# A prefetch hint for the branch that skips the fallback path of a gated-recurrence and feed-forward kernel

## The chip, the core and the metric

The kernel runs on one core of one Trainium2 chip. The metric is the device time of one execution in microseconds. A comparison of two kernels uses the median of several executions of each. The profiled execution is one more execution, recorded instruction by instruction, and has a time of its own.

## What is computed

The reference has two parts. The first is a gated linear recurrence over 768 steps for 4 batches of 8 heads with 48 channels, with a complex gate per step and channel. The second is a feed-forward block on the 3072 rows that result.

```python
def _attn_ref(q, k, v, a_re, a_im):
    mag = np.sqrt(a_re * a_re + a_im * a_im)
    scale = np.minimum(mag, 0.999) / (mag + 1e-06)
    a_re_n, a_im_n = (a_re * scale, a_im * scale)
    for t in range(S):
        ar, ai = (a_re_n[:, :, t, :, None], a_im_n[:, :, t, :, None])
        new_re = ar * S_re - ai * S_im
        new_im = ar * S_im + ai * S_re
        kv = np.einsum('bhd,bhe->bhde', k[:, :, t], v[:, :, t])
        S_re, S_im = (new_re + kv, new_im)
        y[:, :, t] = np.einsum('bhd,bhde->bhe', q[:, :, t], S_re)

def _moe_ref(x, w_in, w_out):          # x: 3072 x 384, w_in: 384 x 2048, w_out: 2048 x 384
    h = x @ w_in
    g = h * (1.0 / (1.0 + np.exp(-h)))
    return (g @ w_out).astype(np.float32)
```

## The kernel before, in words

**Tiling.** The sequence is cut into 24 chunks of 128 steps (6 for each of the 4 batches), and these are handled in 12 pairs. Inside a chunk the recurrence is turned into matrix products: the gates are brought into logarithm and angle, summed along the chunk, and applied to q and k. Then come the products of q and k (L501), the state carried to the next chunk (L574), and the output of the chunk (L525, L528). Each pair gives 256 rows for the feed-forward block. `hidden` (L591) computes the hidden layer in eight groups. `result_of_halves` (L677) multiplies it by the second weight, in a form with seven products of half size for each pair of blocks. VectorE forms sums of the hidden layer for that (L620).

**Order.** The first pairs are written out by hand. The later ones run through `step`, which follows a string of letters, inside a region in which every engine issues its instructions in the order written (`tc.manual_schedule`, L943 and the lines after). Where the instructions written outside that region fall among those inside it is left to the scheduler. The last step, p = 12, has no further chunk to prepare. It computes only the last pair's hidden layer and result, and between these it loads the small parts of the weights that `look` inspects (`small`, L240, and `looked_at`, L247).

**The very end of the arithmetic.** `result_of_halves` ends with one copy on ScalarE (L685), seven adds on VectorE (L689) and three stores to the output: one from SP's queue, one from ScalarE's queue, and a second from SP's queue (all L648).

**The fallback and its branch.** The fast form works only if the decays and the weights are not too small. Behind the region of ordered steps the kernel reduces both to a flag. `low` (L952, L954) is taken from the decays, `fit` (L956, L957) from the weights. Two small DMAs put both in one row (L959, L960), a third reduction gives `weak` (L962), and all five engines load the flag into a register (L964). `tc.If` at L965 runs `step_by_step`, a slow exact path, if the flag is zero. With the inputs of the reference it is not zero, and every engine branches over that code to the end of the program. The skipped code has loops and transfers on SP, VectorE, ScalarE and TensorE, and little on GpSimd. Behind it are only the closing semaphore operations and barriers, which the profile gives the lines L965 and L1119.

```python
    weak = consts.tile([1, 1], I32)
    nc.vector.tensor_reduce(out=weak, in_=all_, op=ALU.min, axis=mybir.AxisListType.X)
    fast.close()
    ok = nc.values_load(weak[0:1, 0:1], min_val=0, max_val=1)
    with tc.If(ok < 1):
        step_by_step(ctx, tc, q, k, v, a_re, a_im, w_in, w_out, w1, w2, out)
```

Of the kernel before, what the change touches and what calls it, by code (L numbers as in the profile page):

```python
# [60 lines left out]
def kernel(  # L61
# [886 lines left out]
            step(p, parts(hidden, p - 1), parts(result, p - 1), order)  # L948


    low = consts.tile([D2, 1], F32)
    nc.vector.tensor_reduce(out=low, in_=decs.rearrange("p n h -> p (n h)"), op=ALU.min,  # L952
                            axis=mybir.AxisListType.X)
# [7 lines left out]
    weak = consts.tile([1, 1], I32)  # L961
    nc.vector.tensor_reduce(out=weak, in_=all_, op=ALU.min, axis=mybir.AxisListType.X)  # L962
    fast.close()
    ok = nc.values_load(weak[0:1, 0:1], min_val=0, max_val=1)  # L964
    with tc.If(ok < 1):  # L965
        step_by_step(ctx, tc, q, k, v, a_re, a_im, w_in, w_out, w1, w2, out)


# [155 lines left out]
```

## Time and profile before

| what | us |
|---|---|
| median of 5 executions | 674.1 |
| lowest and highest of the 5 | 673.02 and 676.2 |
| the profiled execution's own time | 671.09 |
| its span, first to last instruction | 669.3 |
| TensorE busy (matmul) | 638.8 |
| VectorE, ScalarE, GpSimd busy | 454.7, 345.5, 166.8 |
| mean granted TensorE clock | 0.989 of full speed |

In the profile PE is the matmul side of TensorE, PEld its weight loads, DVE is VectorE, ACT ScalarE, POOL GpSimd and SP SyncE. A name with a q behind it (SPq, PEldq) is that engine's sequencer, which handles register, branch, semaphore and DMA-issuing instructions; these are not counted as busy time. The span leaves out what lies before the first and after the last recorded instruction; for this execution that is 1.8 us. Times of single instructions count from the start of the span.

### The profile page before, as it was taken

To read this page: it belongs to the slowest core of one execution; us is meant where nothing else is said; L and a number is where in the kernel's file an instruction comes from. 1 tells how busy PE (TensorE), PEld (TensorE's weight loads), DVE (VectorE), ACT (ScalarE), POOL (GpSimd) and SP (SyncE) were. 2 spreads that over 40 slices of the span, in tenths; PEclk is the share of its full clock that TensorE was granted. 3 is DMA by queue.
4 is the path that set the end of the run, shared out by engine and by line. 5 is a ranking of instruction groups with operands and counts; after the bars stand their busy time and mean duration, and the time that the engine had idled before them with its cause. 6 is when DMAs were issued, how large, how long until landed. Compare 5 with 4: busy or idle time off the path is not lost.

```text
span 669.3 us, 11275 instructions
## 1 busy us (share of the span) xinstructions
PE 638.8 (95%) x4066; PEld 569.9 (85%) x4066; DVE 454.7 (68%) x979; ACT 345.5 (52%) x526; POOL 166.8 (25%) x256
## 2 busy tenths in 40 slices
PE   5688999999999999999999999999999999998995
PEld 3476877577899999999999999999999999997995
DVE  3786736849785784784784784785785785864532
ACT  7779634655862672671681681780780681510110
POOL 7474201250320330230240240240240240230000
PEclk8899999999999999999999999999999999999998
DMA  9968658181294184194185185176176174577730
GB/s 170 226 141 183 147 151 187 39 132 28 42 136 67 36 131 77 35 133 75 30 131 82 33 121 93 31 113 101 30 104 111 32 96 71 195 159 221 232 105 29
DMA packets 171632, 71.20 MB, mean 106 GB/s; under 512 B 155920, under 2 KB 160144, under 8 KB 171568
## 3 DMA queue, kind: packets, MB, share of 16 engines
q1 hardware_dynamic: 158448, 49.76, 37.3%
q0 software_dynamic: 8768, 15.92, 15.7%
q10 hardware_dynamic: 4352, 4.72, 2.1%
q8 instruction: 34, 0.56, 0.3%
q14 instruction: 30, 0.25, 0.1%
HBM read 48.86 MB, written 4.79 MB: 80 GB/s over the span
## 4 chain that ended last, share of the span: by engine, by line
PE 83%; DVE 4%; ACT 4%; DMA 4%; SPq 2%; issue 1%; POOL 0%; DVEq 0%; ACTq 0%
PE h L591 34%; PE o L677 27%; PE a L501 5%; PE o L633 4%; PE s L574 4%; PE y L525 3%; PE y L528 3%; DMA raw<-in_moe_w_in_dram 2%; DMA T<-sq 1%; SPq L492 1%; PE phase L390 1%; ACT s L295 1%; ACT T L483 1%; PE L L390 1%; ACT cs L295 1%
## 5 line engine op out<-in xcount | busy, mean ns | idle before, releaser
L591 PE MATMUL h<-xT,w 128*128 128x256 f32 x1152 | 260.1, 380 | 1.1 <-ACT xT L565 1.1
L591 PEld LDWEIGHTS h<-xT,w 128*128 128x128 f32 x1152 | 216.4, 190 | 29.6 <-ACT xT L565 1.7
L295 ACT ACTIVATE g<-h 128x512 f32<-128x512 f32 x96 | 55.5, 596 | 167.4 <-PE h L591 161.3
L492 POOL DMA_DIRECT2D T<-sq x120 | 77.1, 650 | 65.7 <-issue 56.2
L290 ACT ACT_TABLE_LOAD x64 | 82.1, 1283 | 2.5 <-PEq L1108 1.3
L677 PE MATMUL o<-w,gs 128*128 128x192 f32 x320 | 77.8, 326 | 0.0
L506 DVE TENSOR_TENSOR w<-a,upto_r 128x512 f32<-128x512 f32 x48 | 32.7, 687 | 60.2 <-PE a L501 60.2
L542 POOL DMA_DIRECT2D xT<-y x30 | 15.9, 535 | 213.2 <-ACT y L538 194.2
L677 PE MATMUL o<-w,g 128*128 128x192 f32 x320 | 66.6, 331 | 0.0
L677 PE MATMUL o<-wc,gs 128*128 128x192 f32 x320 | 64.9, 326 | 0.0
L534 ACT COPY xT<-y 128x384 f32<-128x384 f32 x20 | 9.6, 479 | 101.9 <-PE y L528 101.9
L677 PEld LDWEIGHTS o<-w,g 128*128 128x128 f32 x320 | 53.8, 190 | 3.5 <-issue 1.9
L677 PEld LDWEIGHTS o<-w,gs 128*128 128x128 f32 x320 | 56.3, 190 | 0.0
L501 PEld LDWEIGHTS a<-T 96*128 96x128 f32 x384 | 49.1, 192 | 7.4 <-issue 3.2
L677 PEld LDWEIGHTS o<-wc,gs 128*128 128x128 f32 x320 | 54.2, 190 | 0.0
L501 PE MATMUL a<-T 96*128 96x128 f32 x384 | 50.2, 276 | 4.0 <-DMA T<-sq 2.6
L440 POOL DMA_DIRECT2D decs<-ends x48 | 30.5, 641 | 90.8 <-DMA ends<-eq 89.9
L620 DVE TENSOR_TENSOR gs<-g 128x128 f32<-128x128 f32 x160 | 38.6, 282 | 20.9 <-PE o L677 12.8
L633 PE MATMUL o<-w,g 128*128 128x384 f32 x128 | 42.6, 488 | 0.0
L677 PE MATMUL o<-wc,g 128*128 128x192 f32 x160 | 38.9, 326 | 0.0
L633 PEld LDWEIGHTS o<-w,g 128*128 128x128 f32 x128 | 24.2, 190 | 16.1 <-issue 0.2
L525 PE MATMUL y<-w,v 128*64 128x128 f32 x320 | 35.2, 282 | 0.0
(106 smaller groups left out, 947.2 us busy)
## 6 DMA issues: line engine op xcount, KB each, us to landing
T<-sq SPq DMA_DIRECT2D x120, 64.0 KB
T<-sq POOLq DMA_DIRECT2D x120, 64.0 KB, 4.1
raw<-in_moe_w_out_dram SPq DMA_DIRECT2D x16, 384.0 KB
small<-in_moe_w_in_dram SPq DMA_DIRECT2D x16, 384.0 KB
small<-in_moe_w_out_dram SPq DMA_DIRECT2D x16, 384.0 KB
raw<-in_moe_w_in_dram SPq DMA_DIRECT2D x24, 192.0 KB
out_dram<-ot ACTq DMA_DIRECT2D x23, 192.0 KB
q<-in_q_dram SPq DMA_DIRECT2D x18, 192.0 KB
```

What stands on the lines that cost most here:

```text
L290: chain(nc.scalar.preload_act_table_set({"exp": "natural_log_exp_and_others", "trig": "trig_and_small", "silu": "silu_and_others"}[of]))
L295: chain(nc.scalar.activation(out=out, in_=in_, func=func, **kw))
L440: nc.gpsimd.dma_start(out=decs[a * D:(a + 1) * D, n], in_=ends[n].rearrange("(h d) -> d h", d=D))
L492: (nc.gpsimd if a % 2 else nc.sync).dma_start(out=to[ts(b, Q), :, a], in_=sq[ts(a, Q), b])
L501: nc.tensor.matmul(ps[:, h], lhsT=x["kT"][:, hh * HH + h], rhs=x["qT"][:, hh * HH + h], start=True, stop=True)
L506: nc.vector.tensor_tensor(out=x["w", hh], in0=ps, in1=upto.unsqueeze(1).to_broadcast([C, HH, C]), op=ALU.mult)
L525: nc.tensor.matmul(to, lhsT=v_[:, cols], rhs=x["w", h // HH][:, h % HH], start=True, stop=not carried)
L574: nc.tensor.matmul(ps[:, h], lhsT=x["kr"][:, h].rearrange("p c d -> p (c d)"), rhs=x["v"][:, h], start=True, stop=True)
L591: nc.tensor.matmul(ps[:, ji], lhsT=w1[:, dc, ts(jp * 2 + ji, C)], rhs=A[p]["xT"][:, dc], start=(dc == 0), stop=(dc == ND - 1))
L620: nc.vector.tensor_tensor(out=t[:, i], in0=a, in1=b, op=op)
L633: nc.tensor.matmul(A[p]["o"][m].rearrange("p n c -> p (n c)"), lhsT=A[p]["g", jp][:, ji, ts(m, C)], rhs=w2[:, j], start=(j == 0), stop=(j ...
L677: nc.tensor.matmul(o[i], lhsT=a, rhs=b, start=(jp == 0 and i < 4), stop=(final and j == jp and i in ((5, 3, 6, 2) if p == NP - 1 else (4, ...
```

## The change

A call ahead of the reductions marks a place for a branch hint under the name "weak", of the kind "LikelyTaken", on four engines: SP, VectorE, ScalarE and TensorE. The branch of the `If` gets the same name as its label, which ties the two together: at the marked place each of the four engines gets an instruction that names its branch at L965 as one that will probably be taken. GpSimd gets none. Nothing else differs.

```diff
+    tc.mark_branch_hint_location("weak", "LikelyTaken", (
+        mybir.EngineType.SP, mybir.EngineType.DVE, mybir.EngineType.Activation,
+        mybir.EngineType.PE))
     low = consts.tile([D2, 1], F32)
     nc.vector.tensor_reduce(out=low, in_=decs.rearrange("p n h -> p (n h)"), op=ALU.min,
                             axis=mybir.AxisListType.X)
...
     ok = nc.values_load(weak[0:1, 0:1], min_val=0, max_val=1)
-    with tc.If(ok < 1):
+    with tc.If(ok < 1, label="weak"):
         step_by_step(ctx, tc, q, k, v, a_re, a_im, w_in, w_out, w1, w2, out)
```

## The prediction

> **What bounds the kernel now.** I read the page first, then the chain of waits, then the instructions of the two lines at the branch (L964 reads the flag, L965 jumps), then the DMA queues in short stretches around them. From the page:
>
> ```profile
> span 669.3 us, 11275 instructions
> ...
> PE 638.8 (95%) x4066; PEld 569.9 (85%) x4066; DVE 454.7 (68%) x979; ACT 345.5 (52%) x526; POOL 166.8 (25%) x256
> ...
> PE 83%; DVE 4%; ACT 4%; DMA 4%; SPq 2%; issue 1%; POOL 0%; DVEq 0%; ACTq 0%
> ```
>
> TensorE bounds the body, and the change removes no matmul. But its last matmul ends at about 662.4 us and the last VectorE add (L689) at 662.8, while the span ends at 669.3. So 6.5 us lie behind the arithmetic, and the change can act only there. The answer for L965 shows what fills them (columns: engine and operation, count, min/median/max ns, first and last start):
>
> ```profile
> L965 SPq EVENT_SEMAPHORE  x8: 17/17/17, 667.0 to 667.6; - x8
> L965 POOLq COMPARE_BRANCH  x1: 62/62/62, 649.8 to 649.8; - x1
> L965 POOLq EVENT_SEMAPHORE  x1: 17/17/17, 650.3 to 650.3; - x1
> L965 PEldq COMPARE_BRANCH  x1: 3622/3622/3622, 659.9 to 659.9; - x1
> L965 DVEq COMPARE_BRANCH  x1: 72/72/72, 663.1 to 663.1; - x1
> L965 SPq COMPARE_BRANCH  x1: 45/45/45, 663.2 to 663.2; - x1
> L965 ACTq COMPARE_BRANCH  x1: 54/54/54, 663.4 to 663.4; - x1
> ...
> L965 DVEq EVENT_SEMAPHORE  x1: 21/21/21, 666.9 to 666.9; - x1
> L965 ACTq EVENT_SEMAPHORE  x1: 17/17/17, 667.0 to 667.0; - x1
> ```
>
> DVE, SP and ACT branch at 663.1, 663.2 and 663.4, and none issues its next instruction before 666.9 to 667.0: 3.5 to 3.8 us of nothing. TensorE shows the same length inside its branch (3622 ns), but 3.5 us earlier, beside its own queued matmuls. POOL, whose part of the skipped code is small, goes on after 0.5 us. The waits of SP's queue name the same gap, and the DMA answer for 664 to 665 us shows what happens in it:
>
> ```profile
> SPq L965 <- SPq L965: 3.8, 1, 3.8
> ```
>
> ```profile
> DMA  8996864310000700900007000000000000000000
> ...
> q1 hardware_dynamic: 80, 0.05, 16.0%
> q14 instruction: 3, 0.02, 7.3%
> q8 instruction: 1, 0.02, 6.3%
> ```
>
> Each digit of the DMA line is 25 ns. The stores' last data are gone by 664.23; at 664.33 to 664.53 three packets of the instruction queue follow, one for each of the three waiting engines. I read the gap as each engine fetching the code at the branch's target. TensorE's single packet (queue q8) at 661.2 fits too: 1.3 us after its branch, and 2.3 us before it goes on at 663.5.
>
> [...] the branches here took 45 to 72 ns, and I use those. [...] the 0.5 KB transfer of `fit` ended its issue at 647.36, moved data until 648.2, and its reader `weak` started at 648.80. [...]
>
> **The change, part by part.** Nothing is removed or moved in the arithmetic, no wait is added, no DMA is issued by the kernel. Two edits:
>
> 1. The label on the `If`: no instruction, cost nothing.
>
> 2. Four hint instructions, one each on SP, DVE, ACT and PE. No row of before shows one. The nearest rows are single sequencer instructions: a MOVE takes 29 to 42 ns (L1108), L964's register operation 196 ns and its load of the flag 474 to 572 ns. So one hint costs between 0.03 and 0.6 us of its own sequencer; I take 0.1. On PE the sequencer runs ahead of the array (its flag load is at 659.3, the last matmul begins at 662.1), and SP, DVE and ACT idle between their instructions for microseconds at a time. With that cover gone, on DVE behind the last add, it would be 0.1, at most 0.6.
>
> What the hint can take away is the 3.5 to 3.8 us on three engines. All three must lose it, as they resume together. The branch then costs what POOL's costs, 0.5 us from its start to the next instruction: ACT, the latest, is through at 663.4 + 0.5 = 663.9 instead of 667.0, so 3.1 us are the ceiling.
>
> What is late next: the output stores. SP issues the last one at 662.82 for 0.35 us, its data end at 664.23, and SP must see it landed before the kernel may end. The receipt is not visible, because SP arrives too late to wait for it. Two estimates: data end plus the 0.6 us seen for `fit` gives 664.8[...]. I take 665.0. Behind it stand SP's eight semaphore instructions of L965 (667.0 to 667.6) and the closing barrier of L1119 (667.7 to 669.3, 1.6 to 1.7 us). If the wait for the store is the first of the eight, the remaining 2.3 us follow it: end 667.3, gain 2.0. If it is the last, 1.7 us follow: end 666.7, gain 2.6. If it stands later, in the closing barrier, the gain nears 3.1. I take **2.4 us**: span 666.9, and the profiled execution, 671.09 us with 1.8 us around its span, becomes 668.7. The median of the five runs stands 3.0 us above the profiled execution, at 674.1; the same 2.4 us off it gives **671.7 us**, 0.36% less. About 0.3%, or 2.0 us, is what a measurement of this kernel can tell from no change.
>
> The open term is whether the hint acts in time: it must be executed before its engine needs the block, some 3.6 us ahead. In the source it stands behind the ordered steps. It depends on no data, and the trace shows that such code is moved up: `low` (L952), written just behind it, ran at 586.4, between instructions of those steps, as soon as its data were there. Against it, the flag loads, ready at 649.2, sit at 662.4 on DVE and 662.8 on ACT, behind all other work.
>
> **The rivals.**
>
> *Too late or without effect: no change.* If DVE executes its hint just before its flag load at 662.4, the fetch starts there: 662.4 + 3.6 = 666.0 instead of 666.9, gain 0.8; ACT, at 662.8, gains 0.6 and, being the slower, sets it. If nothing is fetched the gain is 0. Median 673.5 to 674.1. For it: the late flag loads, and a gain that needs three engines at once. Against it: `low` moved up by 76 us.
>
> *The hint displaces the block needed next: slower.* If a hint executed early makes the engine fetch the far target at once in place of the code that follows, the engine misses its own next block, 3.6 us, and the target is gone again by the end. Place: VectorE or ScalarE in the start-up, where the chain passes through them; a miss on TensorE is partly covered by the 2.8 us its sequencer was ahead. One uncovered miss: 674.1 + 3.6 = 677.7. It decides from where under 1.6 us of it is hidden. [...] Against it: the code between hint and branch is straight, and a hint names a branch, so it has reason to act only near that.
>
> *The stores bind harder.* Receipts of 2.5 us behind the data would leave an end like today's: gain 0 to 1.5, inside the no-change case.
>
> **How the numbers follow.** In time and effective: 0.62, of which 0.07 ends at a gain under 2.0 us. Too late, without effect, or bound by the stores: 0.27. Displacing: 0.11. That gives faster by over 0.3% 0.55, within 0.3% 0.34, slower 0.11. The likeliest case's own range is a gain of 2.0 to 3.1, 671.0 to 672.1, and medians of five runs that reach from 673.0 to 676.2 may stand a microsecond off: 670.0 to 673.1. The 80% range adds the no-change case with the same spread above it and leaves out most of the slower one: 670.0 to 675.3.
>
> **What the profile after would show.** Right: four new sequencer instructions well before 655 us; PE's branch far under 3622 ns; DVE, SP and ACT with 0.5 us or less from branch to next instruction; SP's L965 group beginning near 663.7 and stretched by a wait for the store until about 665.0; the closing barrier as long as now; the three instruction packets before 663. Too late: hints at 662 and the gap merely shorter. Displaced: a new idle stretch of 3 to 4 us in an engine's sequencer near its hint, and the gap at L965 unchanged. The prediction is wrong if the gap goes and the span doesn't fall by 2 us, or if the span falls elsewhere than behind 662.8.

## The result and the profile after

The changed kernel takes 670.1 us (median of 23 executions), the kernel before 673.45 us (median of 44). The ratio is 0.9946, 95% interval 0.9932 to 0.9961, so 3.6 us are gone (2.6 to 4.6); the two medians themselves lie 3.3 us apart. The forecast was a gain of 2.4 us.

The line numbers of the end have moved by three: the flag loads are L967, the branch L968, the closing barrier L1122. The answer for L968 of the changed kernel (engine and operation, count, min/median/max ns, first and last start) stands against the one for L965 in the prediction:

```profile
L968 SPq EVENT_SEMAPHORE  x8: 17/17/17, 666.3 to 667.6; - x8
...
L968 PEldq COMPARE_BRANCH  x1: 393/393/393, 662.5 to 662.5; - x1
...
L968 DVEq COMPARE_BRANCH  x1: 84/84/84, 665.7 to 665.7; - x1
L968 SPq COMPARE_BRANCH  x1: 70/70/70, 665.8 to 665.8; - x1
L968 ACTq COMPARE_BRANCH  x1: 68/68/68, 665.9 to 665.9; - x1
L968 DVEq EVENT_SEMAPHORE  x1: 21/21/21, 666.3 to 666.3; - x1
L968 ACTq EVENT_SEMAPHORE  x1: 17/17/17, 666.4 to 666.4; - x1
```

TensorE's branch went from 3622 to 393 ns, and DVE, SP and ACT go on 0.5 to 0.6 us after the start of their branches instead of 3.7 to 3.8. SP's eight semaphore instructions now stretch over 1.2 us instead of 0.6. The waits of SP's queue say why (columns: total us, number of waits, the longest):

```profile
SPq L968 <- SPq L968: 1.4, 3, 0.6
```

The first of the three is the rest of the branch, 0.5 us. The other two stand ahead of the second and the third of the eight instructions. The first three of these wait on the semaphores of the three output stores (the trace gives each store's semaphore with its issue), and the last five follow without a gap. The third, for the last store, ends its wait at 667.20, 1.8 us behind the last add. So the landing of the last store is waited for inside this group, but not at its end.

The hints themselves are in the answer for L1122, at the very start of the program:

```profile
L1122 ACTq BRANCH_PREFETCH_HINT  x1: 50/50/50, 0.8 to 0.8; - x1
L1122 SPq BRANCH_PREFETCH_HINT  x1: 65/65/65, 0.8 to 0.8; - x1
L1122 DVEq BRANCH_PREFETCH_HINT  x1: 51/51/51, 0.8 to 0.8; - x1
L1122 PEldq BRANCH_PREFETCH_HINT  x1: 50/50/50, 0.9 to 0.9; - x1
```

The scheduler put them at 0.8 to 0.9 us, over 660 us ahead of the branches (662.5 to 665.9), and they work from there. They fetch nothing at that place. Up to 640 us the trace has 21 packets of the instruction queue q14 and 31 of q8 in both kernels, the first at 32 us. In the whole span the page counts 27 packets of q14 and 33 of q8, where before it was 30 and 34: the extra fetches behind the branch are no longer made. For SP, DVE and ACT the code at the target probably comes in with the only three packets of q14 between 640 us and the branches (651.4, 653.8 and 659.4), where before has three as well (650.7, 650.9 and 656.8). Behind the branches before has six of q14, the changed kernel three. This is inferred; a packet doesn't say what it holds.

But the span of this profiled execution is the same as before:

```profile
span 669.3 us, 11279 instructions
```

I call **tail** the time from the end of the last VectorE add (L689) to the end of the span, and **body** all that is ahead of it. The answers for L689, before and after, with the start of the last add as the last time:

```profile
L689 DVE TENSOR_TENSOR ot<-o,ot x70: 345/348/358, 218.9 to 662.4; 128x192 f32<-128x192 f32 x70
```

```profile
L689 DVE TENSOR_TENSOR ot<-o,ot x70: 345/348/358, 219.8 to 665.0; 128x192 f32<-128x192 f32 x70
```

Before, the add ended at 662.79 and the tail took 6.5 us. Here it ended at 665.37 and the tail took 3.9. In this pair of executions the tail's gain was hidden by a body that was 2.6 us longer; the repeats below show that bodies of one kernel differ by as much. So two questions went to the chip: which parts of the tail's gain come from which engine, and where the gain that is larger than the tail's comes from.

### The profile page after: what moved, and what is told of

It reads as the page before. It is cut to its first block, busy times and chain, and to the rows that moved or that the text cites. A ratio compares the mean times of both kernels' runs of the same rounds, so it can differ in the third digit from the quotient of the medians.

```text
span 669.3 us, 11279 instructions
## 1 busy us (share of the span) xinstructions
PE 642.9 (96%) x4066; PEld 573.5 (86%) x4066; DVE 455.0 (68%) x979; ACT 344.9 (52%) x526; POOL 164.7 (25%) x256
## 4 chain that ended last, share of the span: by engine, by line
PE 83%; DMA 6%; ACT 4%; DVE 3%; SPq 2%; issue 1%; POOL 1%; ACTq 0%; DVEq 0%
PE h L591 34%; PE o L677 27%; PE a L501 5%; PE o L633 4%; PE s L574 4%; PE y L525 3%; PE y L528 3%; DMA q<-in_q_dram 2%; DMA T<-sq 1%; SPq L492 1%; PE phase L390 1%; ACT s L295 1%; DMA raw<-in_moe_w_in_dram 1%; PE L L390 1%; ACT T L483 1%
## 5 line engine op out<-in xcount | busy, mean ns | idle before, releaser
L620 DVE TENSOR_TENSOR gs<-g 128x128 f32<-128x128 f32 x160 | 38.5, 282 | 20.5 <-PE o L677 12.4
```

The lines of the kernel that those rows point to most:

```text
L620: nc.vector.tensor_tensor(out=t[:, i], in0=a, in1=b, op=op)
```

## The experiments

Two theories. **A**: the whole gain lies in the tail, and what is measured beyond it is scatter of the body. **B**: the hints also shorten the body, by about 1 us. Gains below are one minus the ratio, times the median of before in the same comparison, with the interval in brackets; tails are of one profiled execution each.

### The changed kernel again: e1_hint_again, e8_hint_third

No edit.

> The changed kernel once more, beside the kernel before on one chip. Theory A (the whole gain lies behind the last add, the rest of the 3.6 us seen is scatter of the body from run to run): ratio 0.9961, 2.6 us, the tail from the last add to the end 3.9 us instead of 6.5. Theory B (the four hints also shorten the body by about 1 us, through the start or the layout of the code): ratio 0.9946 again, 3.6 us.

> The changed kernel a third time, to place its ratio more narrowly. Theory A: 0.9961. Theory B: 0.9947, as in the two measurements so far.

Measured: 0.9948 (0.9932 to 0.9965), 3.5 us [2.4 to 4.6], tail 3.9 us; and 0.9947 (0.9927 to 0.9968), 3.6 us [2.2 to 4.9], tail 3.9 us. The tail hardly varies, and the ratio repeats. These two alone speak for B's number. The bodies of these executions of one and the same kernel differ, though: the last add ended at 665.37, 662.95 and 664.10. The stretches of the profile around 611 us show one place where that comes from (columns: length, busy time and number of instructions of PE, PEld, DVE, ACT, POOL, then the granted clock, the DMA share and GB/s). First the changed kernel's first profile, then e1_hint_again:

```profile
611.00:612.00 1.00, 1.00 (x13) 1.00 (x11) 0.28 (x2) 0.00 (x0) 0.00 (x0) 0.50 1.02 393
612.00:613.00 1.00, 1.00 (x12) 0.80 (x8) 1.00 (x3) 0.00 (x0) 0.00 (x0) 0.50 0.90 341
```

```profile
611.00:612.00 1.00, 1.00 (x11) 0.81 (x7) 0.31 (x1) 0.65 (x2) 0.00 (x0) 1.00 1.02 384
```

At the same place one execution runs at half clock and the other at full clock. Ahead of it TensorE had stood still in both, for 2.8 and 2.5 us (16 us less the busy time from 600 to 616 us), waiting for the transposing DMAs of the last pair. The waits of the changed kernel's first profile from 600 to 612 us:

```profile
PEld a L501 <- issue: 3.2, 1, 3.2
PE a L501 <- DMA T<-sq: 2.8, 1, 2.8
```

### The kernel before, twice more: e9_before_again, e10_before_third

No edit; a profile each.

> The kernel before, profiled a second time, for the spread of its tail (last add to end), of which there is one sample, 6.5 us. If the fetches behind the branch vary from run to run, the tail lies between 6 and 7.5 us; a tail of 7 us or more would carry most of the gain that is unexplained (3.6 us measured over three comparisons against 2.6 us in the tails). If it is again 6.4 to 6.6, the rest must come from the body.

> The same, a third profile. The body is expected to differ by 1 to 3 us between these two and the first, by the TensorE clock in the start and near 608 to 614 us, where some profiles of one kernel show half clock and others none.

Measured: tails of 6.5 and 5.7 us, last add at 663.69 and 665.72. So the three tails of before average 6.2 us (6.5, 6.5, 5.7), those of the changed kernel 3.9: the tail gives 2.3 us, between 1.8 and 2.6. And the three bodies of before end on average at 664.07, those of the changed kernel at 664.14: the profiled executions show no difference of the body. By their scatter each of these averages is uncertain by about 0.8 us, so a difference of 1 us isn't excluded. The short tail is e10_before_third, where SP resumed earlier than in the others, 3.0 us after its branch:

```profile
L965 SPq EVENT_SEMAPHORE  x8: 17/17/17, 669.1 to 669.7; - x8
...
L965 SPq COMPARE_BRANCH  x1: 45/45/45, 666.1 to 666.1; - x1
```

### Which engine's hint gives what: e2_no_act, e5_no_sp, e6_sp_only, e7_pe_only

The edit is the list of engines of the marked place; for the first:

```diff
-        mybir.EngineType.SP, mybir.EngineType.DVE, mybir.EngineType.Activation,
-        mybir.EngineType.PE))
+        mybir.EngineType.SP, mybir.EngineType.DVE, mybir.EngineType.PE))
```

> Hints on SP, DVE and PE, none on ACT. The tail should be bound by ACT alone, which branches last: ACT's gap of 3.5 to 3.8 us stays, DVE's and SP's shrink to 0.5, and the tail stays at 6.3 to 6.5 us. Theory A: ratio 0.9995 to 1.000. Theory B: the shift of the body stays with three of four hints, ratio about 0.9985. If one engine's gap did not matter: 0.996.

> Hints on DVE, ACT and PE, none on SP. SP alone has work in series behind its branch (eight semaphore instructions, then its part of the closing barrier, 2.3 us in all). Its lone fetch should take about the 3.0 us that ACT's took alone in e2_no_act, so SP resumes 0.6 to 0.8 us earlier than before and the tail is 5.7 to 6.5 us (before 6.5). Theory A (gain only behind the last add): 0 to 0.8 us, ratio 0.999 to 1.000. Theory B (hints at the start shorten the body by about 1 us): 1 to 1.8 us, ratio 0.9975 to 0.9985.

> A hint on SP alone. SP passes its branch in 0.5 us and does its eight semaphore instructions while DVE and ACT still wait for their code; these resume about 3.6 us behind their branch, and then only the closing barrier is left, 1.0 us in e2_no_act. Tail 4.9 to 5.3 us, gain behind the last add 1.2 to 1.6 us: theory A ratio 0.998, theory B 0.9965. If all three engines were needed, as the prediction had it, the tail stays at 6.5 us.

> A hint on PE alone. PE's branch shrinks from 3.6 to 0.4 us, but PE is through before the last add either way, so the tail stays at 6.5 us. Theory A: 1.000. Theory B, if the body gains from PE's hint: 0.9985.

| hints on | ratio (interval) | gain, us | tail, us |
|---|---|---|---|
| SP, DVE, PE | 0.9963 (0.9946 to 0.9980) | 2.5 | 4.5 |
| DVE, ACT, PE | 0.9973 (0.9957 to 0.9990) | 1.8 | 5.2 |
| SP | 0.9989 (0.9967 to 1.0011) | 0.7 | 5.4 |
| PE | 0.9992 (0.9978 to 1.0007) | 0.5 | 5.4 |

The intervals of the last two include no change at all, so these two are read from the profiles alone.

The first expectation missed: without ACT's hint the tail was 4.5 us, not 6.3 to 6.5. ACT does resume late, 3.0 us after its branch, and the others don't. From the answers of e2_no_act for the branch and for the waits of SP's queue:

```profile
L967 SPq EVENT_SEMAPHORE  x8: 17/17/17, 664.6 to 665.9; - x8
...
L967 ACTq COMPARE_BRANCH  x1: 54/54/54, 664.2 to 664.2; - x1
...
L967 ACTq EVENT_SEMAPHORE  x1: 17/17/17, 667.2 to 667.2; - x1
```

```profile
SPq L1121 <- ACTq L967: 0.7, 1, 0.7
```

Meanwhile SP has done its eight semaphores, the wait for the last store among them, and ACT's lateness costs only the 0.7 us by which SP then waits in the closing barrier. Without SP's hint (e5_no_sp) the whole of SP's work stands behind its fetch instead. The tail was 5.2 us, under the 5.7 to 6.5 expected, because SP's gap took 2.5 us and not 3.0:

```profile
L967 SPq EVENT_SEMAPHORE  x8: 17/17/17, 667.8 to 668.4; - x8
...
L967 SPq COMPARE_BRANCH  x1: 45/45/45, 665.3 to 665.3; - x1
```

All profiles with a branch agree with one sum. Measured from the last add, the end is the latest of three: SP's first instruction behind the branch plus 2.24 us; ACT's plus 1.0 us (DVE's never was the last); the end of SP's wait for the last store, at 1.8, plus 2.05 us. Before: 4.25 + 2.24 = 6.5. SP alone hinted: ACT's 4.4 + 1.0 = 5.4. All hinted: 1.83 + 2.05 = 3.9.

With PE's hint alone I had expected a tail of 6.5 us; it came to 5.4. TensorE was through long before, but the other engines' gaps were shorter:

```profile
L967 SPq EVENT_SEMAPHORE  x8: 17/17/17, 670.7 to 671.2; - x8
...
L967 PEldq COMPARE_BRANCH  x1: 398/398/398, 664.6 to 664.6; - x1
...
L967 SPq COMPARE_BRANCH  x1: 45/45/45, 667.9 to 667.9; - x1
```

The five unhinted gaps in runs with a working hint on PE took 2.5 to 3.0 us; the nineteen in runs without one, the three profiles of before among them, took 3.0 to 4.1. That TensorE's own late fetch gets in the way of the others is my guess and was not shown. One of the unhinted tails is 5.7 us, so the 5.4 us of this one profile don't show a gain by themselves.

For theory B: B wanted the extra 1 us wherever hints stand at the start. Gains beyond the tail (taken against the 6.2 us of before) are 0.8 us for SP, DVE, PE; 0.8 for DVE, ACT, PE; -0.1 for SP; -0.3 for PE. Each interval is about 1 us or more to either side, so these four don't decide.

### A late hint: e3_hint_at_650

```diff
-    tc.mark_branch_hint_location("weak", "LikelyTaken", (
...
     ok = nc.values_load(weak[0:1, 0:1], min_val=0, max_val=1)
+    tc.mark_branch_hint_location("weak", 1 - ok, (
+        mybir.EngineType.SP, mybir.EngineType.DVE, mybir.EngineType.Activation,
+        mybir.EngineType.PE))
```

> The hint takes its kind from the flag's register (1 - ok, zero for taken), so it stands behind the flag loads, which the scheduler then puts near 650 to 654 us on SP, DVE and ACT and behind the last matmul on PE. Nothing is added at the start. If a hint acts [...] some 9 to 12 us ahead, the gaps on SP, DVE and ACT are 0.5 us, the tail 3.9 us, the gain 2.6 us (0.9961) under theory A and the same under B, unless B's extra comes from the start, where 0.9961 stands against 0.9946 of the changed kernel. [...] the gaps stay at 3.5 us and the ratio is 0.9995, less the flag loads' 0.5 us that leave the tail.

Measured: 0.9988 (0.9971 to 1.0005), tail 6.0 us. The hints of this run, and its branch:

```profile
L1122 ACTq BRANCH_PREFETCH_HINT  x1: 54/54/54, 652.9 to 652.9; - x1
L1122 DVEq BRANCH_PREFETCH_HINT  x1: 55/55/55, 653.0 to 653.0; - x1
L1122 SPq BRANCH_PREFETCH_HINT  x1: 63/63/63, 653.6 to 653.6; - x1
L1122 PEldq BRANCH_PREFETCH_HINT  x1: 49/49/49, 663.1 to 663.1; - x1
```

```profile
L968 SPq EVENT_SEMAPHORE  x8: 17/17/17, 669.6 to 670.1; - x8
...
L968 PEldq COMPARE_BRANCH  x1: 3378/3378/3378, 663.2 to 663.2; - x1
L968 DVEq COMPARE_BRANCH  x1: 84/84/84, 665.4 to 665.4; - x1
L968 ACTq COMPARE_BRANCH  x1: 73/73/73, 665.8 to 665.8; - x1
L968 DVEq EVENT_SEMAPHORE  x1: 21/21/21, 666.0 to 666.0; - x1
L968 SPq COMPARE_BRANCH  x1: 70/70/70, 666.2 to 666.2; - x1
...
L968 ACTq EVENT_SEMAPHORE  x1: 17/17/17, 669.4 to 669.4; - x1
```

The result is mixed. DVE's hint at 653.0 worked (0.6 us from branch to next instruction). ACT's at 652.9 and SP's at 653.6 did not, though they stood 12.6 to 12.9 us ahead of the branch (gaps of 3.6 and 3.4 us); TensorE's, 0.1 us ahead, did not. Of the two outcomes expected, all three gaps at 0.5 us or all three at 3.5, neither came. So time ahead of the branch is not what decides: SP's hint stood 0.2 us further ahead of its branch than DVE's, and ACT's 0.5 us. What does decide was not shown. The instruction queue q14 shows two packets at 654.0 to 654.25 us and one at 659.5 to 659.75. If the packet at 659.5 was DVE's, it came 6.5 us behind DVE's hint, but the packets don't name their engine. The tail of 6.0 us is bound by SP, as the sum above has it (3.8 + 2.2).

### No branch at all: e4_no_branch

```diff
-    ok = nc.values_load(weak[0:1, 0:1], min_val=0, max_val=1)
-    with tc.If(ok < 1):
-        step_by_step(ctx, tc, q, k, v, a_re, a_im, w_in, w_out, w1, w2, out)
```

> The fallback path, its branch and the flag loads are left out (the flag is still computed). Nothing to fetch out of order and no load behind the last add: the tail is what the stores and the closing barrier need. If the changed kernel is bound by the landing of the last store, this one has the same tail, 3.8 to 3.9 us, and the ratio of theory A, 0.996; if the branch, 0.5 us a piece, or the flag loads still cost something, the tail is 3.2 to 3.5 us, ratio 0.995.

Measured: 0.9965 (0.9948 to 0.9981), 2.4 us, tail 3.2 us. The tail is 0.7 us shorter than with the hints. The wait for the last store ends no earlier (1.9 us behind the last add, against 1.8), but SP then executes five more semaphore instructions before its closing drains, where the changed kernel has seventeen. So what the fallback still costs here lies in SP's semaphore instructions, not in the flag loads or the branch. Yet the run is not faster than the changed kernel. Its gain is 0.7 us smaller than its tail says (against 6.2 us before), the changed kernel's 1.3 us larger. Its profile has one of the two longest half-clock stretches near 611 us (mean granted clock 0.57 from 608 to 616 us, as in e7_pe_only, against 0.79 in the six other profiles with such a stretch), with the last product of q and k at 618.2 instead of 614.2 us. The body's chance is as large as the effects looked for.

### A body without the 3 us wait: e11_looks_later, e12_looks_later_hint, e13_looks_sooner, e14_looks_sooner_hint, e15_looks_later_hint

To take away the wait ahead of the half clock, the loads that look at the weights (`look`, 384 KB each) begin only behind the last transposes (`tB` of step 11), so that the transposing DMAs don't queue among them. In e13 and e14 the first look only starts three loads. The comments that name runs are not in the code:

```diff
+        turned_both = p >= NP
         for x in order.split():
             if x in what:
                 what[x]()
-            if x in "hr" and p + 1 >= NP:
+            turned_both = turned_both or x == "tB"
+            if x in "hr" and p + 1 >= NP and turned_both:
                 look()
...
             for n in range(3):
                 small(n)
+            return                                    # e13, e14
-        for _ in range(1 + (len(looks) % 6 == 0)):
+        for _ in range(1 + (len(looks) % 3 == 0)):    # e11, e12, e15; % 2 in e13, e14
```

> No hint. The 384 KB loads that look at the weights begin only behind the last transposes of k and q (about 600 us), a few more per part afterwards, so that the transposing DMAs of the last pair don't queue behind them. In the profiles TensorE stood for 3 us near 605 to 608 waiting for these DMAs, and in some came back at half clock. If that wait goes, the body is 3 to 5 us shorter and the runs scatter less; if the loads then crowd the end, the flag comes later than 662 us and the kernel gets slower. The tail stays at 6.5 us.

> The same with the hint on all four engines. Theory A: 2.6 us less than e11_looks_later, all of it in the tail (3.9 instead of 6.5 us), since the body has no chance event left that the hint could shift. Theory B: 3.6 us less. If e11_looks_later is faster than before, this is the fastest of all, ratio 0.988 to 0.991.

> As e11_looks_later, without hint, but the first look only starts three loads and waits for none, and the later ones load more each, so the flag should be there before 655 us. No TensorE wait near 605 us, no half clock there. Tail 5.7 to 6.5 us; last add at 661 to 662; median 669 to 670, ratio 0.994 to 0.9955.

> The same with the four hints. Theory A: the body as in e13_looks_sooner within the scatter (0.5 us), the tail 3.9 us, so 1.8 to 2.6 us less in all, ratio 0.9905 to 0.992. Theory B: 3.6 us less, ratio 0.989.

> e12_looks_later_hint again: 667.5 us, ratio 0.9905. Its late flag costs a tail of 4.3 instead of 3.9 us, so e14_looks_sooner_hint should be up to 0.4 us faster.

| run | hints | median, us (executions) | ratio (interval) | tail, us |
|---|---|---|---|---|
| e11_looks_later | none | 670.6 (22) | 0.9965 (0.9948 to 0.9981) | 7.5 |
| e12_looks_later_hint | four | 667.5 (6) | 0.9905 (0.9874 to 0.9935) | 4.3 |
| e15_looks_later_hint | four | 667.0 (7) | 0.9929 (0.9902 to 0.9956) | 4.3 |
| e13_looks_sooner | none | 668.2 (19) | 0.9945 (0.9930 to 0.9959) | 5.9 |
| e14_looks_sooner_hint | four | 666.2 (6) | 0.9905 (0.9880 to 0.9929) | 3.9 |

The long wait is gone in all five profiles: from 600 to 616 us TensorE is idle for 1.2, 0.2, 0.7, 0.0 and 0.0 us, in the order of the table, in the twelve others for 2.3 to 3.3. The half clock near 611 us is gone in all five too (granted clock 1.00 from 600 to 616 us); in eight of the twelve others it was there. The stretch in which the kernels above stood, in e14_looks_sooner_hint:

```profile
606.00:608.00 2.00, 2.00 (x33) 1.88 (x34) 1.12 (x2) 0.23 (x1) 0.00 (x0) 1.00 0.86 257
```

In e11 the flag comes too late, the branches start 1.1 to 1.5 us behind the last add instead of 0.3 to 0.6, and the tail grows to 7.5 us; e13 mends that. The pairs were to answer the question. From e13 to e14 the median falls by 2.0 us (the mean by 2.6) and the tail by 2.0. From e11 to e12, on one chip, the median falls by 3.1 us (the mean by 3.4) and the tail by 3.3. By the ratios the two steps are 2.7 and 4.0 us, 0.7 to 0.8 us more than the tails. e15_looks_later_hint, the repeat of e12 on another chip, fell short of the 0.9905 expected. With six executions for each of e12 and e14 a step is uncertain by about 1 us to either side, estimated from the scatter. So the pairs agree with theory A, but they don't rule out B's extra 1 us. e14_looks_sooner_hint has the lowest median of the study, 6.4 us below before by its ratio (4.8 to 8.1), and the changed kernel's tail.

## Why the prediction was right or wrong

**The gap as a fetch, and the hint as its cure: right.** Gaps of 3.7 to 3.8 us became 0.5 to 0.6, about what POOL's branch had cost before (0.5); that they were fetches is inferred from the packets of q14 behind the branches, three instead of six; the hint's own price, taken as 0.1 us, was 50 to 65 ns at 0.8 us.

**Placement: right.** The hints were moved up like `low`, and further. But 3.6 us ahead of the branch, which the prediction asked for, isn't enough by itself: in e3_hint_at_650 the hints of SP and ACT stood 12.6 and 12.9 us ahead and had no effect.

**What is late next: the total right, its parts not, which is part luck.** The prediction had the last store seen landed 2.2 us behind the last add (665.0 against 662.79) and took, between 1.7 and 2.3, some 1.9 us for what follows: a tail of 4.1 us. The tail was 3.9. But the wait for the store ended at 1.8, and as it is the third of the eight, 2.05 us follow it. One term was 0.4 us too long, the other 0.15 too short. Of the 2.2 us, 1.4 lead to the end of the store's data (664.23 in the profile of before), 0.6 are what `fit` took from the end of its data to its reader, and 0.2 were added as an estimate. Here the wait ended 1.8 us behind the start of the issue, 1.5 us behind its end and 0.4 us behind the end of the data. The central 2.4 us lies within the 1.8 to 2.6 us that the three profiles of before give.

**"All three must lose it, as they resume together": wrong.** That they resumed within about 0.1 us of each other was chance: in the two further profiles of before they resumed 0.9 and 1.1 us apart. SP's lateness costs in full, ACT's only what it exceeds SP's other work by, 0.6 us in e2_no_act.

**The displacing rival: refuted.** A hint 660 us ahead fetches nothing by itself (21 and 31 packets up to 640 us, as before), leaves no new idle stretch and still works. **The too-late rival: real elsewhere.** It did not occur in the change. In e3_hint_at_650 PE's hint, 0.1 us ahead, was too late (its branch took 3378 ns), and those of SP and ACT, over 12 us ahead, were without effect.

**The sum: the failing step is "the same 2.4 us off" the median of five.** It had two terms, and both were mis-sized. The five-run median, 674.1, stood 0.65 us above the median of 44 executions, 673.45; measured from there, 671.7 us was a forecast of only 1.75 us. And the step took the body as constant. In the first pair of profiles the gap went and the span stayed at 669.3 us, which the prediction had named as a sign of being wrong; a body 2.6 us longer was the reason. Executions of before end their body anywhere in 2.9 us (662.79 to 665.72). In the three comparisons of the changed kernel the gain was 3.5 to 3.6 us. Of this the tail gives 2.3, near the forecast, and 1.2 to 1.3 us lie beyond it, where the prediction had nothing. The lower ends of the three intervals (2.6, 2.4 and 2.2 us) reach or nearly reach the tail's 2.3. But three comparisons that agree, 0.9946 to 0.9948, are hard to take as mere scatter.

The recorded clock says where a good part of it may lie. The mean granted clock was 0.9876 for the changed kernel against 0.9844 for before in e1_hint_again, and 0.9871 against 0.9838 in e8_hint_third. Over the span that is 4.4 and 4.5 us less at half clock. The shorter tail, whose end TensorE spends idle at half clock (the last 3.9 us in the first profile of before, the last 0.5 us in that of the changed kernel), accounts for 2.3 to 2.6 us of this, an estimate from the profiles; some 2 us are left for the body. Within the four sets of executions of before whose clock is recorded, each us at half clock goes with a span longer by 0.25 to 0.45 us, and by arithmetic work at half speed would lose 0.5. So the 2 us are worth 0.5 to 1.0 us, as an estimate. Whether the hints bring this about or chance did stays open: the profiled bodies and the two pairs with later looks are too few to tell.

## What to carry to other kernels

When the span ends microseconds after the last arithmetic, look at the branch instructions there: here a jump over a large block cost SP, DVE and ACT 3.0 to 4.0 us each before the change, and a hint executed long before took it away for 50 to 65 ns. Ask of each engine what work stands behind its branch; here SP, with work in series, decided, and the last store, seen landed 1.8 us behind the last add, set the floor. When a change of 2 us is to be judged, take the stretch it acts on from several profiles instead of trusting the sum, because the rest of the kernel can move as much by itself.

## What the runs showed of the hardware that I had not expected

- A branch over the fallback whose hint was missing or had no effect took 2.5 to 4.1 us on SP, DVE and ACT, in runs of nearly the same code: 2.5 to 3.0 where TensorE's hint had worked, 3.0 to 4.1 elsewhere.
- A hint worked from 660 us ahead, without fetching anything there, yet not from 12.6 to 12.9 us ahead on SP and ACT, while DVE's worked from 12.4 us ahead.
- The last store was seen landed 1.5 us behind the end of its issue, 0.4 us behind the end of its data.
- After standing for 2.8 us TensorE came back at half clock in the changed kernel's first profile (granted clock 0.50 from 611 to 614 us), after 2.5 us at full clock in e1_hint_again, the same kernel. Before e9_before_again's full clock it stood for 3.3 us, the longest of all.
